# Attention and top-1 MoE in one kernel: first transfers in a fixed order, modality words by GpSimd, last keys' values two pairs at a time, and a planner's transfer figures fitted anew

## The chip, the cores and the metric

The kernel runs on one core of one Trainium2 chip. The metric is the device time of one execution in microseconds (us); the median of several runs is compared. A core has TensorE (PE, matrix products), VectorE (DVE), ScalarE (ACT), GpSimd (POOL) and SyncE (SP, which only issues DMAs and reads registers here). ACT and GpSimd can issue DMAs too.

## The reference

```python
scale = 1.0 / np.sqrt(64)                        # q, k, v: 8 x 8 heads x 576 x 64, tau = 0.02
scores = scale * np.matmul(q, k.transpose(0, 1, 3, 2))
thresh = np.max(scores, axis=-1, keepdims=True) - tau
scores = np.where(scores >= thresh, scores, -1000000000.0)
attn = np.exp(scores - np.max(scores, axis=-1, keepdims=True))
attn = attn / (np.sum(attn, axis=-1, keepdims=True) + 1e-09)
x = np.matmul(attn, v) ...                       # heads side by side: 4608 x 512
logits = x @ w_gate + modality_bias[modality_id] # 4608 x 8; modality_id is an 8-byte integer, 0 or 1
e_idx = np.argmax(logits, axis=1)
probs = np.exp(logits - logits.max(-1, keepdims=True))
probs /= probs.sum(-1, keepdims=True) + 1e-09
for e in range(8):                               # out = 0 before
    mask = e_idx == e
    h = np.maximum(x[mask] @ w1[e], 0.0)         # w1: 8 x 512 x 1024
    out[mask] = gate_w[mask, None] * (h @ w2[e]) # w2: 8 x 1024 x 512; gate_w = probs at e_idx
```

## The kernel before

The kernel has no order of its own in its text. Each step (an instruction or a few on one engine) is recorded in a `Plan` with its engine, an assumed duration, what it reads and writes, and a due time. `order()` then runs a list schedule through these assumed durations: on each engine the ready step that is due first goes next. The instructions are written out in that order, and each engine works through its own list strictly in order. Four figures, `LAND`, say how the planner expects a DMA to land: a lead, a pace for each unit of the transfer's size, a latency, and a floor for GpSimd's transfers. A transfer's size is given by hand as `us`, and every `load` takes 0.6 us of its issuing engine. `fill()` puts products of zeros where the plan expects TensorE to idle for over 0.6 us (L1435). A packed table of bytes, `SHIFTS`, moves each step's due time by up to 8 us either way; it has one byte for each step, so it belongs to one list of steps.

*Attention.* 64 heads are worked on as 32 pairs, each in 9 steps of 128 query rows: 288 steps. A step: TensorE makes the scores (L827) into one of two buffers `s` (576 keys, the last 64 of them from `nk` and `qb`); VectorE takes the row maximum `nm` (L836, L838); ACT takes the exponent `e` (L842); VectorE masks and sums to `pr` (L854); TensorE transposes `pr` (L880), ACT copies that to `ptm` (L883). The last 64 keys of two steps go through `rp` (copied by GpSimd, L867, or ACT) and `ptr` (L893, L900). TensorE multiplies with the values (L761): `v_m` holds 512 of a head's 576 rows of v, `vr` the last 64. For the first pair q and k come in parts, `raw` (512 rows of one head, halves of the columns) and `y` (the last 64 rows of both heads), transposed by TensorE (L768, L761, L787) and split by ACT and VectorE into high and low halves (`km`, `q`, L755, L757, L781, L783). Later pairs come as `kq`, are transposed on TensorE (L692) or VectorE, and are split by GpSimd (L727, L729, L749).

*Routing and experts.* After each batch the gate is computed, and a table of rows by expert, `tab`, is scattered. The words `modality_id` enter once, near the start: `xg` from DRAM, cast by VectorE to `y` (L644, L645). In the stream of attention stand 8 slots of expert work, and 4 more behind it: SyncE reads the expert's number and the rows (`tb`), GpSimd gathers rows of x (L1160, `xg`, `txg` behind the attention) and scales them (`xn`, L1182; VectorE behind the attention), TensorE transposes (L1187), SyncE loads weights (`raw`), GpSimd splits them (L1221, L1223), TensorE does both layers (L1239, L1271), ACT and VectorE hold the hidden layer's halves (`hh`, `hl` L1253), and GpSimd stores the result (L1290). Which slots are run behind the attention is computed on VectorE (L1060 to L1126, `le` and others).

All plain loads go through `load`, at L488. TensorE's results go to banks `bk`, `pm` or score buffers `s`; a matmul that reuses a bank waits until the bank's last reader is done.

## Time and profile before

| | us |
|---|---|
| runs | 999.27, 999.71, 1003.33 |
| median | 999.71 |
| profiled execution, its own time | 1002.75 |
| its span, first to last instruction | 1000.9 |
| busy: PE, DVE, ACT, POOL | 961.2, 747.2, 614.3, 593.8 |
| TensorE's mean granted clock | 0.988 |

Rows of the trace below come from the profiled execution. In a row of a time line the first number is the start, the second the length, then engine, line, operation, what it writes and reads, how many instructions stand together, and in brackets how long the engine had been idle before and what released it.

### The profile page before, as it was taken

Reading aid. Unit: us, or ns where it says so; the run is one execution under the profiler, and the core shown is the slowest. Engines: PE = TensorE matmul, PEld = TensorE weight load, DVE = VectorE, ACT = ScalarE, POOL = GpSimd, SP = SyncE. Lnnn points to the kernel's source line nnn. Section 1 sums busy time; section 2 is a strip of 40 time slices with the busy share of each in tenths; the row PEclk is TensorE's granted clock in tenths of the full one; section 3 lists DMA queues with packets and bytes.
Section 4 is the critical chain, followed back from the end, with each engine's and each line's share of the span. In section 5 each row is a group of like instructions: output and inputs, shape, how many; then the busy total and the mean of one; then the engine's idle time right before and its main releaser. Section 6 shows DMA issues by size and latency. Waiting matters only on the chain.

```text
span 1000.9 us, 19578 instructions
## 1 busy us (share of the span) xinstructions
PE 961.2 (96%) x6304; PEld 768.8 (77%) x6304; DVE 747.2 (75%) x1792; ACT 614.3 (61%) x1256; POOL 593.8 (59%) x746
## 2 busy tenths in 40 slices
...
GB/s 162 167 192 183 196 189 191 169 204 185 182 140 194 191 193 128 185 183 167 148 158 200 178 171 147 179 142 186 190 136 87 97 199 200 116 104 103 142 63 28
DMA packets 310448, 159.58 MB, mean 159 GB/s; under 512 B 235902, under 2 KB 281982, under 8 KB 308416
## 3 DMA queue, kind: packets, MB, share of 16 engines
...
q10 hardware_dynamic: 2112, 0.52, 0.2%
...
HBM read 85.98 MB, written 20.73 MB: 107 GB/s over the span
## 4 chain that ended last, share of the span: by engine, by line
PE 48%; DVE 5%; issue 3%; POOL 2%; ACT 1%; another core or an unknown queue 0%; POOLq 0%; ACTq 0%; DVEq 0%
PE bk L1239 11%; PE bk L1271 11%; PE bk L761 7%; PE s L827 7%; PE bk L880 5%; PE pm L1271 3%; PE pm L1239 1%; PE bk L1187 1%; DVE pr L854 1%; DVE nm L836 1%; DVE xn L1182 1%; DVE le L1090 1%; PE bk L893 1%; POOL out_dram L1290 0%; PE bk L961 0%
## 5 line engine op out<-in xcount | busy, mean ns | idle before, releaser
L842 ACT ACTIVATE e<-s,nm 128x576 f32<-128x576 f32 x288 | 213.9, 746 | 73.6 <-DVE nm L836 67.9
L854 DVE SCALAR_TENSOR_TENSOR pr<-s,nm,e 128x576 f32<-128x576 f32 x288 | 231.3, 812 | 28.8 <-ACT e L842 10.2
L836 DVE TENSOR_REDUCE nm<-s 128x1 f32<-128x576 f32 x288 | 214.8, 749 | 30.7 <-PE s L827 25.3
L827 PE MATMUL s<-km,q 128*128 128x288 f32 x1024 | 190.9, 313 | 7.0 <-DVE pr L854 5.0
L883 ACT COPY ptm<-bk 128x512 f32<-128x512 f32 x256 | 146.3, 592 | 45.3 <-PE bk L880 37.0
L827 PEld LDWEIGHTS s<-km,q 128*128 128x128 f32 x1024 | 147.5, 189 | 34.4 <-DVE pr L854 14.0
L880 PE MATMUL bk<-ident,pr 128*128 128x128 f32 x1152 | 166.4, 275 | 1.4 <-DVE hl L1253 1.4
L880 PEld LDWEIGHTS bk<-ident,pr 128*128 128x128 f32 x1152 | 136.6, 141 | 19.1 <-issue 2.9
L761 PE MATMUL bk<-ptm,v_m 128*64 128x256 f32 (+1 forms) x1024 | 139.7, 417 | 2.3 <-ACT ptr L900 2.3
L761 PEld LDWEIGHTS bk<-ptm,v_m 128*64 128x64 f32 x1024 | 69.2, 138 | 53.6 <-issue 11.1
L1253 DVE SCALAR_TENSOR_TENSOR hl<-bk,hh 128x512 fp32r<-128x512 f32 (+3 forms) x78 | 45.9, 591 | 64.3 <-ACT hh L1251 64.1
L1239 PE MATMUL bk<-xh,w1h 128*128 128x512 f32 (+2 forms) x240 | 89.7, 374 | 0.2
L729 POOL TENSOR_TENSOR q<-kqt,q 128x576 fp32r<-128x576 f32 x62 | 88.0, 1423 | 2.3
L1271 PE MATMUL bk<-w2h,hh 128*128 128x512 f32 x200 | 84.7, 423 | 0.0
L1239 PE MATMUL bk<-xh,w1l 128*128 128x512 f32 (+2 forms) x240 | 83.8, 349 | 0.4 <-POOL w1l L1223 0.4
L1223 POOL TENSOR_TENSOR w1l<-raw,w1h 128x512 fp32r<-128x512 f32 x64 | 82.3, 1288 | 2.9
L1239 PE MATMUL bk<-xl,w1h 128*128 128x512 f32 (+2 forms) x240 | 83.6, 348 | 0.0
L1223 POOL TENSOR_TENSOR w2l<-raw,w2h 128x512 fp32r<-128x512 f32 x64 | 81.9, 1284 | 2.2
L1271 PE MATMUL bk<-w2l,hh 128*128 128x512 f32 x200 | 79.5, 398 | 2.0 <-POOL w2l L1223 2.0
L727 POOL CAST q<-kqt 128x576 fp32r<-128x576 f32 x62 | 41.0, 668 | 65.0 <-PE s L827 36.7
L1271 PE MATMUL bk<-w2h,hl 128*128 128x512 f32 x200 | 79.1, 396 | 0.0
L1290 POOL DMA_INDIRECT out_dram<-y,tb x37 | 38.2, 1034 | 61.8 <-DVE y L1283 46.1
...
## 6 DMA issues: line engine op xcount, KB each, us to landing
raw<-in_moe_w_dram SPq DMA_DIRECT2D x128, 256.0 KB
...
```

What stands on the lines that cost most here:

```text
L729: op("POOL", 1.425, lambda s=s: nc.gpsimd.tensor_tensor(out=q2[:, 1, s], in0=kqt[:, s], in1=f32(q2[:, 0, s]), op=ALU.subtract), [kqt[:, s] ...
L761: nc.tensor.matmul(out=o, lhsT=lhsT, rhs=rhs, start=start, stop=stop, skip_group_check=True)
L827: nc.tensor.matmul(out=g.t[:, hf, 0:SH], lhsT=a, rhs=x, start=(z == 0), stop=(z == len(passes) - 1))
L836: op("DVE", 0.757, lambda: nc.vector.tensor_reduce(out=nm[:, 0, x:x + 1], in_=g.t[:, :, 0:SH], axis=AX.XY, op=ALU.max, negate=True), [g], ...
L842: op("ACT", 0.747, lambda: nc.scalar.activation(out=e, in_=g.t[:, :, 0:SH], func=AF.Exp, bias=nm[:, 0, x:x + 1]), [g, nm[:, 0, x:x + 1]], ...
L854: op("DVE", 0.826, lambda: nc.vector.scalar_tensor_tensor(out=pr.rearrange("p (a x) -> p a x", a=2), in0=g.t[:, :, 0:SH], scalar=nm[:, 1, ...
L880: op("PE", 0.44, lambda: [nc.tensor.transpose(out=g.t[:, kc * P:(kc + 1) * P], in_=pr[:, kc * P:(kc + 1) * P], identity=ident) for kc in r ...
L883: op("ACT", 0.583, lambda: nc.scalar.copy(out=o, in_=g.t.rearrange("a (k p) -> a k p", p=P)), [g], [o])
L1223: op("DVE" if d else "POOL", 0.686 if d else 1.29, lambda: (nc.vector if d else nc.gpsimd).tensor_tensor(out=lo.t, in0=raw.t, in1=f32(hi.t ...
L1239: nc.tensor.matmul(out=g.t[:, 0:WT], lhsT=a.t[:, cs], rhs=x.t[:, c, 0:WT], start=(c == 0 and y == 0), stop=(c == KC - 1 and y == 2))
L1253: op("DVE", 0.1 + 0.58 * WT / 512, lambda: nc.vector.scalar_tensor_tensor(out=hl.t[:, 0:WT], in0=g.t[:, 0:WT], scalar=0.0, in1=f32(hh.t[:, ...
L1271: nc.tensor.matmul(out=g.t, lhsT=a.t[:, ts], rhs=w.t, start=(y == 0 and i == 0), stop=(y == F2 - 1 and i == 2))
```

## The change

Four loads of `first` q and k parts by ACT and six by SyncE get due times of their own in the order in which they are written: k then q of the first head columns, then the few rows of k, then the second k and q parts, then the few rows of q. The modality words are loaded by GpSimd, in five transfers of one 4-byte word for each row (128 x 8 words), instead of nine by SyncE with both words of the 8 bytes. The last 64 rows of v come for two pairs in one transfer for each head of a pair: 32 transfers instead of 64. The planner's figures for landing, issuing and for some steps change, a wait `WAKE` is added where a SyncE instruction waits for a DMA, and `SHIFTS` is a new table.

```diff
-    LAND = (0.2, 1.05, 1.7, 4.5)
+    LAND = (0.0, 1.0, 1.95, 4.9)
+    WAKE = 0.7
...
+                x.soon = max(x.soon, fin + (self.NEXT if same else self.LAT).get(o.eng, 0.0 if same else 0.04)
+                                    + (self.WAKE if o.dma is not None and x.eng == "SP" else 0.0))
...
+    ISSUE = {0.1: 0.8, 0.2: 0.75, 0.6: 0.66, 0.95: 0.72, 1.3: 0.58, 2.6: 0.56}
+
     def load(out, in_, rd=(), wr=(), us=1.0, due=None, eng="SP"):
         q_ = {"SP": nc.sync, "ACT": nc.scalar, "POOL": nc.gpsimd}[eng]
-        op(eng, 0.6, lambda: q_.dma_start(out=out, in_=in_), rd, list(wr) or [out], dma=us, due=due)
+        op(eng, 1.0 if eng == "POOL" else 0.5 if eng == "ACT" else ISSUE.get(us, 0.65), lambda: q_.dma_start(out=out, in_=in_), rd, list(wr) or [out], dma=us, due=due)
...
-    vr2 = tiles(glob, 2, [P, 2, D], F32, "vr")
+    vr4 = keep(glob, [P, 4, D], F32, "vr")
...
+        turn_ = [20.0 * i - 260.0 for i in range(11, -1, -1)]
+
         def part(z, s, x, eng):
             load(first[z][s].t.rearrange("p (c x d) -> p c x d", c=NC, x=2)[:, :, x, :],
-                 (k, q)[z][0, s, 0:SA, :].rearrange("(c p) d -> p c d", c=NC), wr=[(first[z][s], x)], us=0.4, eng=eng)
+                 (k, q)[z][0, s, 0:SA, :].rearrange("(c p) d -> p c d", c=NC), wr=[(first[z][s], x)], us=0.5, eng=eng, due=turn_.pop())
...
-        mid_i = bi.t[:, 0:2 * B * NT].bitcast(I32).rearrange("p (b t two) -> p b t two", b=B, t=NT)
-        mid_v = mid.bitcast(I32).rearrange("(b s two) -> b s two", s=S, two=2)
-        for b in range(B):
-            load(mid_i[:, b, 0:NC, :], mid_v[b, 0:SA, :].rearrange("(c p) two -> p c two", c=NC), wr=[(bi, b)], us=0.4)
-        load(mid_i[:, :, NC, :], mid_v[:, S - P:S, :].rearrange("b p two -> p b two"), wr=[(bi, B)], us=0.7)
+        mid_i = bi.t[:, 0:B * NT].bitcast(I32).rearrange("p (b t) -> p b t", b=B)
+        mid_v = mid.bitcast(I32).rearrange("(b s two) -> b s two", s=S, two=2)[:, :, 0]
+        for t, o in enumerate([*range(0, SA, P), S - P]):
+            load(mid_i[:, :, t], mid_v[:, o:o + P].rearrange("b p -> p b"), wr=[(bi, t)], us=0.5, eng="POOL")
...
-            load(r[s * R:(s + 1) * R], sv[:, SA:S, :].rearrange("s r d -> r s d"), us=0.2)
+
+    def load_vr(p):
+        b, j = p // NPAIR, p % NPAIR
+        if p % 2 == 0:
+            for s in range(2):
+                load(vr4[s * R:(s + 1) * R], v[b, 2 * j:2 * j + 4, SA:S, :].rearrange("s r d -> r s d"), us=0.3)
...
-        op("DVE", 1.35, f1, [lg], [lt, mx])
-        op("DVE", 1.87, f2, [lt, iota_m, iota_x], [fe, mn, oh[:, 0:NT, :]])
+        op("DVE", 1.5, f1, [lg], [lt, mx])
+        op("DVE", 1.2, f2, [lt, iota_m, iota_x], [fe, mn, oh[:, 0:NT, :]])
...
-            op("SP", 0.4, f, keys, [(z, "e")])
+            op("SP", 1.0, f, keys, [(z, "e")])
...
-            op("SP", 0.9, f, keys + ["tab"] + [("tab", b, t) for b in range(nb) for t in range(NT)], [tb], dma=0.4)
+            op("SP", 1.7, f, keys + ["tab"] + [("tab", b, t) for b in range(nb) for t in range(NT)], [tb], dma=0.4)
...
-                eng, dur, e = ("DVE", 1.0, nc.vector) if xt_eng else ("POOL", 1.45, nc.gpsimd)
+                eng, dur, e = ("DVE", 0.77, nc.vector) if xt_eng else ("POOL", 1.2, nc.gpsimd)
...
-                op("SP", 0.42, g, late + [(z, "e")], [raw], dma=0.9)
+                op("SP", 0.65, g, late + [(z, "e")], [raw], dma=1.0)
...
+        at(t0 + 8, lambda p=p: load_vr(p))
...
-        c-k#iXCM^(1OA;&lvFaRH+d<QRgtnIA-i(6oITEV&Yowl<Lu+?jLx3fl7vzyTS}CfS=Qa}|9<#CAD)lTr)McYNexQ&vBBHo{d4OHHd=Oe&n%
+        c-j@!1w&K`+koL`&IAlG)F2^Uf^-f@NOw2V9Rmy?NOz}nr*t>cD1wb(V6N`kxd`Se;Q8L~`Vse?kxk1;$@EJtO)^S0;Vw<eO^eD+ipeXiN=y
```

Some 11 lines are added to the file, so a step that stood at L488 is at L493 after, L761 at L772, L827 at L838, L1182 at L1193 and L1271 at L1282. What the new order does is seen at three places.

The first place is the start. SyncE's first transfers (`raw_81` and `raw_82` hold k, `raw_83` and `raw_84` q, `y_113` and `y_114` the few last rows) are, before:

```order
L488 DMA y_113<-in_k_dram 64x2x64
L488 DMA raw_82<-in_k_dram 128x4x64
L488 DMA raw_83<-in_q_dram 128x4x64
L488 DMA y_114<-in_q_dram 64x2x64
L488 DMA raw_81<-in_k_dram 128x4x64
L488 DMA raw_84<-in_q_dram 128x4x64
```

and after:

```order
L493 DMA raw_81<-in_k_dram 128x4x64
L493 DMA raw_83<-in_q_dram 128x4x64
L493 DMA y_113<-in_k_dram 64x2x64
L493 DMA raw_82<-in_k_dram 128x4x64
L493 DMA raw_84<-in_q_dram 128x4x64
L493 DMA y_114<-in_q_dram 64x2x64
```

TensorE, behind its warm-up on zeros, before:

```order
L761 MATMUL bk_79<-ident,y_113 64x64 x2
L761 MATMUL bk_80<-ident,y_113 64x64 x2
L768 MATMUL bk_78<-ident,raw_83 128x128 x4
L768 MATMUL bk_77<-ident,raw_82 128x128 x4
L768 MATMUL bk_80<-ident,raw_81 128x128 x4
L787 MATMUL bk_79<-ident,y_114 128x64
L768 MATMUL bk_78<-ident,raw_84 128x128 x4
L827 MATMUL s_75<-km_164,q_162 128x288 x4
```

and after:

```order
L779 MATMUL bk_80<-ident,raw_81 128x128 x4
L779 MATMUL bk_79<-ident,raw_83 128x128 x4
L772 MATMUL bk_80<-ident,y_113 64x64 x2
L772 MATMUL bk_78<-ident,y_113 64x64 x2
L779 MATMUL bk_77<-ident,raw_82 128x128 x4
L798 MATMUL bk_79<-ident,y_114 128x64
L838 MATMUL s_75<-km_163,q_161 128x288 x4
L838 MATMUL s_76<-km_163,q_161 128x288 x4
```

The parts of k and q that the first scores read stand ahead of the few rows, and the second q part behind the scores (two rows further on). GpSimd's five word transfers stand ahead of its first copy of `rp`, in two pairs and a single one.

The second place is the second batch's slot of expert work on GpSimd. Before:

```order
L1160 DMA xg_101<-xs,tb_120 128x512
L1160 DMA xg_99<-xs,tb_120 128x512
L727 CAST q_163<-kqt 128x576
L1221 CAST w2h_91<-raw_81 128x512
L1160 DMA xg_100<-xs,tb_120 128x512
L729 TENSOR_TENSOR q_163<-kqt,q_163 128x576
L749 CAST nk<-km_164 64x576
L1182 TENSOR_TENSOR xn_102<-xg_101,tb_120 128x4x64 x2
L1290 DMA out_dram<-y_118,tb_119 4608x512
L1182 TENSOR_TENSOR xn_102<-xg_99,tb_120 128x4x64 x2
```

and after:

```order
L1171 DMA xg_101<-xs,tb_120 128x512
L1171 DMA xg_99<-xs,tb_120 128x512
L1171 DMA xg_100<-xs,tb_120 128x512
L738 CAST q_162<-kqt 128x576 x2
L760 CAST nk<-km_163 64x576
L740 TENSOR_TENSOR q_162<-kqt,q_162 128x576
L1193 TENSOR_TENSOR xn_102<-xg_101,tb_120 128x4x64 x2
L740 TENSOR_TENSOR q_162<-kqt,q_162 128x576
L1193 TENSOR_TENSOR xn_102<-xg_99,tb_120 128x4x64 x2
```

The three gathers now stand together, the second subtraction of `q` comes behind the first `xn`, and the store of an earlier result is not between the first two `xn`.

The third place is VectorE's part of the table of slots behind the attention. Before:

```order
L1085 TENSOR_TENSOR off<-off,ns 1x24
L1086 TENSOR_TENSOR off<-off,cum 1x24
L1090 TENSOR_TENSOR le<-ij,cum 1x88 x3
L1094 TENSOR_REDUCE ej<-le 1x33
L1098 TENSOR_SCALAR em<-ej 1x33
L1100 TENSOR_TENSOR le<-em,iota_m 1x88
L1102 TENSOR_TENSOR le<-le,off 1x88
L1253 SCALAR_TENSOR_TENSOR hl_111<-pm_9050,hh_107 128x512
L1100 TENSOR_TENSOR le<-em,iota_m 1x88
```

and after:

```order
L1096 TENSOR_TENSOR off<-off,ns 1x24
L1097 TENSOR_TENSOR off<-off,cum 1x24
L1101 TENSOR_TENSOR le<-ij,cum 1x88 x3
L1264 SCALAR_TENSOR_TENSOR hl_111<-bk_77,hh_107 128x512
L1105 TENSOR_REDUCE ej<-le 1x33
L1109 TENSOR_SCALAR em<-ej 1x33
L1111 TENSOR_TENSOR le<-em,iota_m 1x88
L1113 TENSOR_TENSOR le<-le,off 1x88
```

The step `hl_111`, which frees a bank, stands directly behind the three `le` now, where four small steps stood between.

## Rows read from the trace of the kernel before

**Rows 1.** The page, busy time of TensorE: us, share of the span, instructions.
```profile
PE 961.2 (96%) x6304; PEld 768.8 (77%) x6304; DVE 747.2 (75%) x1792; ACT 614.3 (61%) x1256; POOL 593.8 (59%) x746
```

**Rows 2.** Busy us by stretch: length, PE, PEld, DVE, ACT, POOL, clock, DMA share, GB/s.
```profile
0.00:25.00 25.00, 19.69 (x158) 17.02 (x158) 16.14 (x48) 15.22 (x31) 9.89 (x40) 1.00 0.75 162
25.00:125.00 100.00, 95.48 (x723) 69.71 (x724) 90.67 (x238) 72.64 (x133) 48.46 (x94) 1.00 0.86 185
760.00:860.00 100.00, 91.14 (x425) 70.25 (x424) 57.15 (x99) 27.30 (x49) 80.49 (x88) 0.95 0.52 144
```

**Rows 3.** TensorE's waits by releaser: us in total, times, the longest.
```profile
PE s L827 <- DVE pr L854: 6.1, 11, 1.3
...
PE bk L761 <- ACT ptr L900: 2.3, 1, 2.3
PE bk L893 <- POOL rp L867: 2.1, 1, 2.1
...
PE bk L692 <- DMA kq<-in_q_dram: 1.2, 1, 1.2
```

**Rows 4.** Time line of TensorE, start: us, us, instruction [idle before, releaser].
```profile
4.62 0.69 PE L761 MATMUL bk<-ident,y 64*64 64x64 f32 x8
7.05 2.79 PE L768 MATMUL bk<-ident,raw 128*128 128x128 f32 x12 [1.74 <-DMA raw<-in_q_dram]
...
10.07 1.10 PE L768 MATMUL bk<-ident,raw 128*128 128x128 f32 x4
11.15 1.44 PE L827 MATMUL s<-km,q 128*128 128x288 f32 x8
```

**Rows 5.** Time line of VectorE, start.
```profile
9.04 0.88 DVE L757 SCALAR_TENSOR_TENSOR q<-bk,gq,q 128x384 fp32r<-128x384 f32 x2 [2.73 <-ACT q L755]
```

**Rows 6.** Time lines of VectorE and then TensorE, 46 to 51 us.
```profile
46.87 1.35 DVE L644 CAST y<-xg 128x40 f32<-128x40 int32 x1 [0.73 <-DMA xg<-in_moe_modality_id_dram]
...
50.23 0.54 PE L827 MATMUL s<-km,q 128*128 128x288 f32 x2 [1.31 <-DVE pr L854]
```

**Rows 7.** Time line of GpSimd, start.
```profile
1.59 0.74 POOL L488 DMA_DIRECT2D tau_b<-in_tau_dram  x1 [0.15 <-issue]
...
15.30 1.27 POOL L727 CAST q<-kqt 128x576 fp32r<-128x576 f32 x2 [9.34 <-ACT kqt L695]
```

**Rows 8.** Time line of SyncE's DMA issues, 37 to 43 us.
```profile
37.47 0.65 SPq L488 DMA_DIRECT2D vr<-in_v_dram  x1
...
39.45 3.48 SPq L488 DMA_DIRECT2D xg<-in_moe_modality_id_dram  x3
```

**Rows 9.** Time lines of GpSimd and then TensorE, 213 to 223 us.
```profile
213.94 1.08 POOL L1160 DMA_INDIRECT xg<-xs,tb  x1 [0.16 <-DMA out_dram<-y,tb]
...
218.79 1.41 POOL L729 TENSOR_TENSOR q<-kqt,q 128x576 fp32r<-128x576 f32 x1
...
220.76 1.18 POOL L1182 TENSOR_TENSOR xn<-xg,tb 128x256 f32<-128x256 f32 x2
...
222.00 0.66 PE L1187 MATMUL bk<-ident,xn 128*128 128x128 f32 x4 [3.39 <-POOL xn L1182]
```

**Rows 10.** Time lines of VectorE, GpSimd and TensorE, 796 to 804 us.
```profile
796.42 5.63 DVE L1090 TENSOR_TENSOR le<-ij,cum 1x88 f32<-1x88 f32 x3
...
802.82 0.24 DVE L1100 TENSOR_TENSOR le<-em,iota_m 1x88 f32<-1x88 f32 x1
...
803.26 0.67 DVE L1253 SCALAR_TENSOR_TENSOR hl<-pm,hh 128x512 fp32r<-128x512 f32 x1
...
799.51 1.29 POOL L1223 TENSOR_TENSOR w1l<-raw,w1h 128x512 fp32r<-128x512 f32 x1
...
803.99 0.80 PE L1271 MATMUL pm<-w2h,hh 128*128 128x512 f32 x1 [3.13 <-DVE hl L1253]
```

**Rows 11.** Time lines of VectorE and then TensorE, 849 to 855 us.
```profile
849.18 5.35 DVE L1182 TENSOR_TENSOR xn<-txg,tb 128x256 f32<-128x256 f32 x2 [0.48 <-PE bk L1187]
...
854.59 1.11 PE L1187 MATMUL bk<-ident,xn 128*128 128x128 f32 x4 [3.30 <-DVE xn L1182]
```

More of the change, by code (lines that the diff above doesn't have):

```diff
@@ L255, in begin @@
                 same = x.eng == o.eng and o.dma is None
-                x.soon = max(x.soon, fin + (self.NEXT if same else self.LAT).get(o.eng, 0.0 if same else 0.04))
+                x.soon = max(x.soon, fin + (self.NEXT if same else self.LAT).get(o.eng, 0.0 if same else 0.04)
+                                    + (self.WAKE if o.dma is not None and x.eng == "SP" else 0.0))
                 x.left -= 1
@@ L292, in order @@
                         same = s.eng == o.eng and o.dma is None
-                        s.ready = max(s.ready, t + (self.NEXT if same else self.LAT).get(o.eng, 0.0 if same else 0.04))
+                        s.ready = max(s.ready, t + (self.NEXT if same else self.LAT).get(o.eng, 0.0 if same else 0.04)
+                                        + (self.WAKE if o.dma is not None and s.eng == "SP" else 0.0))
                         s.n -= 1
@@ L643, in f @@
         def f():
-            nc.vector.tensor_copy(out=mid_f[:, 1, :], in_=mid_i.rearrange("p b t two -> p (b t) two")[:, :, 0])
+            nc.vector.tensor_copy(out=mid_f[:, 1, :], in_=mid_i.rearrange("p b t -> p (b t)"))
             nc.vector.tensor_scalar(out=mid_f[:, 0, :], in0=mid_f[:, 1, :], scalar1=0.0, scalar2=None,
                                     op0=ALU.is_equal)
-        op("DVE", 0.8, f, [(bi, b) for b in range(B + 1)], [bf])
+        op("DVE", 0.8, f, [(bi, t) for t in range(NT)], [bf])
         for m, (t, key) in enumerate(((bias_t, bias_t), (bias_u, bu))):
@@ L653, in late_constants @@
            [bias_t, bu], [bias_t])
-        for b, xs_ in ((bx, [bx]), (bi, [(bi, b) for b in range(B + 1)])):
+        for b, xs_ in ((bx, [bx]), (bi, [(bi, t) for t in range(NT)])):
             op("POOL", 0.45, lambda b=b: nc.gpsimd.memset(b.t, 0.0), wr=xs_ + [b])
@@ L705, in load_v @@
         b, j = p // NPAIR, p % NPAIR
-        t, r = vm2[p % 2], vr2[p % 2]
+        t = vm2[p % 2]
         sv = v[b, 2 * j:2 * j + 2]
@@ L903, in pv @@
     def pv(p):
-        vt, vr = vm2[p % 2], vr2[p % 2]
+        vt, vr = vm2[p % 2], vr4[:, 2 * (p % 2):2 * (p % 2) + 2]
         ot = ot_[p % (NPAIR + 1)]
@@ new lines, in tile_attn_moe @@
+        |@>B;*eJNr*7+B@ZzX_#G&>k>#LK4*F~kZ%fZeoS=wF77r^Yu#vQa^^g|>_@kA{Ui2m=A?`XM9#+B$_Q?UEF@C90{;?jqp;`9JX^F1>ah3rq
+        PQa*MOk!Y6AAD%dEZs0I;mIXA@4Z=*)~tHQ5bNON*O%>ggsHc@K{ZslicCxEF)ADTt-PtJdPdB<?&;ZYb|X_)7u@$s)*obN)%p>nUk{%D&(3
+        inn68N9VbE2DtGmsZd223t?Etl`Zl_cJg_2GYeLC0l=XE}K=vB!q$vV{u@OJrqN@^1}BJ^esjyY(pIl}N_-3Tn(AH}pF7j=sm2*M&Z>7$KFb
+        QO$VUQu3V0UZ1)_7QF_(pFr(XyQ3s1R}|*TP~!0QA+S6U!ra3vCJU3Yw6yC1Q}IMqL4H7tX~8{$ACL?(&o9{C17HJ8Wz}k_EI)cdpee_*bFP
+        f2nntHwY~^Bxy84IPu+&sKq(dy#^VB<>a;KoXw5lnv-Iv!Mmoqc=&MYzQs)$9K2cb^?-F#g*ilT>oF#~ZjSZNXnOVpzGvk_VXRP%2xuI{!qx
@@ new lines, in tile_attn_moe @@
+        o2rV_bSbf1N6jB3?2jo!GJBkB?$!mPS;_6bJ%Y!$u8%KzyI;V?CT1@Zj*TE#4r^;Z+DVh`SA>{Ow+ONnehvjSNWwno=VzQ9CKke=HBABBB;-
+        +<it3;v(~l;_|5~OB4sqBn5RNLu!OuM4yKG`HQ|~F-!E9`63A~Tw~t(`5wYbk341}5N^;1;xAT$48IvLgV!KsKKFR!s}}k2HXNfzHHt#Bhsd
+        0~a!kn;oo1n9AQbQnNMGbyNYOfj55G=;Gz&m0QwZrgrX4VB;3k6*HgEl&M4-=@z=N;E$g#MBL0M!?zp_cN^n;p>skSnM<CDH%SdUJ4&~()`{
+        6MFs&Ojmycr|Sh?M`7#qA;L`+N_gMl&(&10V%#Q0Yd5~DKx;G8DhC4p$;*|5ZuI_DHE$j&<6{Hh^lx|1Rx<_55g;vvtUt13pNuXtj9w9Hyu1
+        sun~KhYM{`0zd8Mn-n*Z_|HVrCil!k)IH$d`(uy_u!Jit`vtqu+s01x%*Jdx3{KhLkJocJR?idmoGEK44Eht^Qnx)R{X)Jg$$khPI4}e66fY
@@ new lines, in tile_attn_moe @@
+        tTi0Ojxz_7F<SUiZUq4F8T{E!p!^@*E}D^g0O6C?bu4R3jn~3seG|4`Qp*U%@GlTH^<37!t}4EY8H_q@%cmyXbESFw_ey06#Z;;9C%6vB&ww
+        A(!vhMZWn(sX>fX;rTB1j>Es5%gI^h+VJw6iH2o6@c>0;9@)HPKRxLd#6?G$t)LGJTC*j+L_AgE_z^BgcfLRe>|bG*f+M|=`F=mR{Oo!l`o`
+        cI(?<L_P6t~bIxn!3Z}pXNPK0ae22yXupuR(3@L5NCDcD70tix0`QlLGZNf`$PH2^Mb?OJ>5UfLg>tBAnC4I_hzv7G309sM4R=h(7)+o*C$8
+        RhZ+k|m7HyozTFfLGC^>^1}^VDVc23>Q{}e^(!HyvW9RqE-A70N9gPS(x(>#SZ&aE9k4bi=b!@dg=Yh?w7~a8buwzE6CKih6o%#^8S_Os<I%
+        qqa6X^{J>C|S{1l?G<rhd8am^e&w;m~(HRADkp(31_-b*e&<!{Gt6$6&`KBlBNUUDl)A?O~IF>G*#U123JZbGMlI({JJ-_t?+=sDXmD7I{X`
```

125 lines of the change are left out of this document (54 added, 71 removed).

## The prediction

> **What bounds the kernel now.** I began with the engines' busy time: TensorE is busy 961.2 us, 96% of the span of 1000.9 [rows 1], so all that any change of order can win is what TensorE loses between its matmuls and after the last: about 40 us. The table by stretch of time says where [rows 2]. The first 25 us lose 5.3 us; from 25 to 125 us, 4.5 are lost, and there VectorE is at 90.67 of 100, so this stage is close to being bound by VectorE; the stretch 760:860, in which the attention has ended and the expert work is left, loses 8.9 us at a mean granted clock of 0.95. The list of TensorE's waits then gives names [rows 3], and its time line the places [rows 4, 9 to 11]: a few waits that occur once, each on another releaser: an xn of GpSimd (3.39 us), an xn of VectorE (3.30), an hl of VectorE (3.13), a ptr of ACT (2.3), an rp of GpSimd (2.1), the first part of q (1.74). Only the wait of the scores (L827) on pr recurs: 11 times, 6.1 us in all. A kernel whose order is planned from assumed durations stalls where an assumption is off by a few us, so I price the change by these places, one by one.
>
> **The change part by part.**
>
> *First transfers.* In the kernel before, the first real matmuls (the few rows of k) end at about 5.3 us, TensorE waits 1.74 us for the first part of q until 7.05, and the first scores run at 11.15 [rows 4]. So from the first part transposed to the first scores there are 11.15 - 7.05 = 4.1 us of ACT and VectorE steps. Both queues now send the parts of k and then q that scores 0 need ahead of everything else, and TensorE transposes them ahead of the few rows. What came first in the old order was in TensorE at 4.62 us, so I estimate that the first parts of k (larger than the few rows) are there at 4.8: the scores then start at 4.8 + 4.1 = 8.9, that is 2.25 us sooner. VectorE's work on q starts at 9.04 [rows 5], and its stage lasts to about 125 us at nine tenths busy [rows 2], so that what it starts sooner it ends sooner. Term: -2.25; bounds 0 (another part is late in its place) and -2.8 (the wait of 1.74 and 1.10 us of four transposes that now follow the scores).
>
> *Modality words.* Nine SyncE transfers become five on GpSimd, of 1024 separate 4-byte words each. What this removes: at 46.87 us VectorE had waited 0.73 us for the words and then spent 1.35 us on the cast, behind which TensorE waited 1.31 us for pr [rows 6]. In the new order the cast stands behind the eighth pr instead, some 25 us sooner, where VectorE is the bound too, so it still costs its own time, and only the wait and what the cast's stride costs can go. Term: -1.0; bounds -2.1 (0.73 + 1.35, all of it) and 0. What it adds: GpSimd's issue time. GpSimd is idle for 9.34 us before 15.30 us [rows 7], and the five stand there. The one plain transfer that GpSimd issues before, tau with 128 words, takes 0.74 us; a gather of 128 rows takes 1.08 [rows 9]. At 1.0 us each, five take 5.0 us inside the idle 9.34: nothing. At 0.74 us per 128 words they would take 8 x 0.74 = 5.9 us each, 29.6 in all, 20 us more than the cover, in front of the rp copies and q casts that the scores need. I take 1.0, since the two rows differ by far less than their bytes do; the upper bound is a rival below. The Trainium skill, "DMA: Bandwidth & Descriptors", section "Anatomy of one DMA", says that descriptor generation is small and variable and that many descriptors can be emitted before the cost shows; by it the five cost nothing beyond their 1.0, and no run here shows it yet.
>
> *SyncE.* Nine word transfers and, by loading the last keys' values for two pairs at once, 32 others go. Three of the word transfers take 3.48 us of SyncE's time, one vr load 0.65 [rows 8], so the loads queued behind the nine words go out up to 9 x 1.16 = 10.4 us sooner. But TensorE waits for such a load once (L692 on kq, 1.2 us [rows 3]), and a load that is hidden anyway wins nothing: term 0, bounds 0 and -1.2.
>
> *New order, second batch's slot.* GpSimd's xn started 6.82 us after the first gather had: two more gathers and the work on the next q stood ahead of it, and TensorE waited 3.39 us [rows 9]. In the new order the three gathers stand together and the second subtraction of q (1.41 us) is put behind xn, but three casts and a subtraction stay ahead, so GpSimd's own way from gather to xn is hardly shorter. What changes is that TensorE now has scores, transposes and l2 matmuls listed between gather and its transposes. Term: -2.0; bounds -3.4 and 0.
>
> *New order, the table of slots.* At 796.42 us three small tensor-tensor steps on VectorE (88 numbers each) take 5.63 us, while the same kind takes 0.24 a little later; GpSimd then runs casts and subtractions without a break. The hl behind them comes at 803.26, and TensorE, which needs its bank, loses 3.13 us [rows 10]. The planned figure of these steps is not touched. In the new order hl2 stands right behind the three; before, 803.26 - 802.05 = 1.2 us of small steps stood between. And the bank is asked for after 18 matmuls where it was 15, which I estimate at 0.6 us. So of 3.13 some 1.3 remain: term -1.8, bounds -3.1 and 0 (what GpSimd does beside it decides). The rule is in the Trainium skill, "SBUF — State Buffer", section "Who interferes with whom": a VectorE instruction with two SBUF inputs and a GpSimd instruction that reads SBUF exclude each other, and the loser waits whole instructions. The trace agrees (5.63 us for three, against 0.24). By that rule alone the stall depends on what GpSimd does just then, and the new figure for VectorE's xn speaks against the change.
>
> *New order, tail xn.* At 849.18 us two VectorE xn take 5.35 us, again beside GpSimd's work, and TensorE loses 3.30 us [rows 11]. The planner's figure for one goes from 1.0 to 0.77, away from these 2.7. In the new order six matmuls stand between the transposes of one chunk and the next, as before, and the two xn between them. Term: 0; bounds -3.3 and +1.
>
> *What a new order brings of its own.* The waits on ptr and rp, 2.3 and 2.1 us, came once each in 32 pairs of the same steps [rows 3]; a new order ends such waits and makes others. I count those two as drawn anew (0), and add 2.3 us, one such wait more, since the places improved above may be followed by others. The amount of matmuls and fillers is unchanged.
>
> **Sum.** -2.25 - 1.0 + 0 - 2.0 - 1.8 + 0 + 2.3 = -4.75 us. Against the profiled execution (1002.75 us, span 1000.9) this is 998.0; the median of the runs before is 999.71, 3.04 us under the profiled one, and against it 995.0. Half a per cent (5.0 us) is about what a measurement can tell from no change here: the three runs of before lie within 4.1 us.
>
> **The rivals.**
> *The stalls are only dealt anew* (0.24). The start wins 2.25, and new waits of two or three us each take it back. For it: nearly all waits of [rows 3] occur once. Against it: two of the figures that are changed (GpSimd's xn, the start of the transfers) lie at named stalls. Time: 998 to 1001.
> *Words by the piece* (slower, 0.08). GpSimd's transfer costs per word. 5 x 5.9 - 9.34 = 20 us late: 1015. It decides from (9.34 + 4.75) / 5 = 2.8 us for each on. Against it: 0.74 for 128 words and 1.08 for 128 rows of 2 KB differ little.
> *More blocked VectorE steps in the expert stage* (slower, 0.09). If xn (planned at 0.77) now meets GpSimd's work in four places of the stretch after 760 us where it was one, 3 x 3.3 = 9.9 us are lost, and at a clock of 0.95 [rows 2] the 100 us behind it some 2 more: 995.0 + 9.9 = 1005 to 1007. It decides from three such new waits on.
> *The fit removes most named waits* (0.14). -2.25, -1.3, -3.4, -3.3, -3.1 and half of ptr's and rp's 4.4 sum to -15.6: 984; with a third given back, 989.
> *My forecast* has the rest, 0.45: between 992 and 998.
>
> **How the numbers follow.** The range reaches from the half-won fit, 987, to the sum with three more waits of 3 us, 1004; outside lie the fullest fit (0.06), the words by the piece (0.08) and the worst of the expert stage (0.06). Faster by over 0.5% means under 994.7: the fit (0.14) and 0.65 of my own case, since more of its bounds lie below the sum than above (0.45 x 0.65 = 0.29): 0.43. Slower is 0.08 + 0.09 = 0.17. The rest, 0.40, is no change.
>
> **What would show it.** Right: the first scores near 8.9 us; no transfer of modality words on SyncE; five GpSimd issues near 1.0 us before 15 us; VectorE's cast without a wait before it; no wait of TensorE over 2 us on xn near 218 us; a wait of some 1.3 us on hl near 797, and one of about 3 us on a VectorE xn near 850. Wrong: first scores at 10.5 or later, GpSimd issues over 2.8 us or several new waits over 2 us in places that are not named here.

## The result and the profile after

The changed kernel takes 1004.26 us (median of 19 runs) beside 998.97 for the kernel before (19 runs on the same chip): ratio 1.0063, 95% interval 1.0044 to 1.0082, a loss of some 6 us. The ratio is that of the mean times, without one slow run of the kernel before (1552.37 us). The profiled execution took 1003.29 us with a span of 1001.6.

The page of the kernel after, busy time; it answers to [rows 1]:

```profile
PE 958.9 (96%) x6303; PEld 766.3 (77%) x6303; DVE 755.4 (75%) x1792; ACT 612.4 (61%) x1256; POOL 596.1 (60%) x751
```

The stretches of after, columns as in [rows 2], with the one that holds the end:

```profile
0.00:25.00 25.00, 19.93 (x151) 17.38 (x153) 17.17 (x50) 15.86 (x34) 16.59 (x47) 0.93 0.82 152
25.00:125.00 100.00, 95.26 (x737) 70.65 (x736) 92.39 (x238) 73.17 (x132) 48.25 (x95) 1.00 0.89 189
...
760.00:860.00 100.00, 90.82 (x418) 70.11 (x415) 55.69 (x100) 26.73 (x47) 81.99 (x89) 0.97 0.53 149
860.00:1001.60 141.60, 131.71 (x622) 109.48 (x621) 52.80 (x85) 44.57 (x81) 47.01 (x55) 0.98 0.30 91
```

In the first three TensorE is busy within 0.4 us of what it was. TensorE's waits of after, as in [rows 3]:

```profile
PE s L838 <- DVE pr L865: 9.8, 15, 1.7
PE bk L1198 <- DVE bj L1120: 3.7, 1, 3.7
PE bk L772 <- DVE oh L1015: 3.4, 3, 2.5
PE bk L1198 <- DVE xn L1193: 3.3, 1, 3.3
PE bk L1198 <- POOL xn L1193: 2.3, 3, 0.9
```

The waits that stood against hl (3.1), rp (2.1) and ptr (2.3) are gone or under 0.7; pr has 3.7 us more, and the waits put down to bj (read below) and oh are new. All listed waits sum to 31.9 us, where they were 32.3. TensorE's time line at the start, as in [rows 4]:

```profile
7.12 0.45 PE L772 MATMUL bk<-ident,y 64*64 64x64 f32 x8 [0.85 <-ACT km L792]
7.50 0.66 PE L779 MATMUL bk<-ident,raw 128*128 128x128 f32 x4
9.11 0.27 PE L798 MATMUL bk<-ident,y 64*128 64x64 f32 x1 [0.95 <-DVE q L768]
9.31 2.21 PE L838 MATMUL s<-km,q 128*128 128x288 f32 x8
```

The first scores start 1.84 us sooner, but their eight matmuls take 2.21 us where they took 1.44, in a stretch whose mean granted clock is 0.93. Time lines of GpSimd at the start and then of VectorE at the cast, as in [rows 6, 7]:

```profile
4.71 1.86 POOL L493 DMA_DIRECT2D xg<-in_moe_modality_id_dram  x2
...
7.38 0.88 POOL L493 DMA_DIRECT2D xg<-in_moe_modality_id_dram  x1
...
8.83 1.75 POOL L493 DMA_DIRECT2D xg<-in_moe_modality_id_dram  x2
13.94 0.24 POOL L878 COPY rp<-pr 128x64 f32<-128x64 f32 x1 [3.36 <-DVE pr L865]
...
26.57 1.07 DVE L650 CAST y<-xg 128x40 f32<-128x40 int32 x1
27.67 0.60 DVE L651 TENSOR_SCALAR y<-y 128x40 f32<-128x40 f32 x1
```

Five issues of about 0.9 us each, all before GpSimd waits anyway, and a cast that waits for nothing. Then the table of slots, VectorE and TensorE, as in [rows 10]:

```profile
797.36 2.44 DVE L1113 TENSOR_TENSOR le<-le,off 1x88 f32<-1x88 f32 x1
799.83 0.42 DVE L1117 TENSOR_REDUCE bj<-le 1x33 f32<-1x264 f32 x1
800.28 2.96 DVE L1118 TENSOR_TENSOR bj<-bj,ij 1x33 f32<-1x33 f32 x1
803.17 0.67 DVE L1264 SCALAR_TENSOR_TENSOR hl<-bk,hh 128x512 fp32r<-128x512 f32 x1
803.77 0.16 DVE L1120 TENSOR_SCALAR bj<-bj 1x33 f32<-1x33 f32 x1
...
803.99 0.63 PE L1198 MATMUL bk<-ident,xn 128*128 128x128 f32 x4 [3.67 <-DVE bj L1120]
```

The blocked steps are others of the same table, and TensorE waits 3.67 us instead of 3.13, at the same time of the program. The view puts this down to bj, which the transposes of xn do not read. In the same trace the record of their wait for VectorE starts at 803.88 us, after hl's semaphore update (803.85) and before bj's (803.94): what TensorE waits for is an hl again, a later one, which reads a bank and stands behind the blocked L1118. Last, the end, which the prediction did not price. TensorE's last instruction and GpSimd's last stores of after:

```profile
991.32 0.39 PE L1282 MATMUL pm<-tw2h,hl 128*128 128x512 f32 x1
992.07 0.98 POOL L1301 DMA_INDIRECT out_dram<-y,tb  x1 [3.90 <-DVE y L1294]
993.35 0.93 POOL L1301 DMA_INDIRECT out_dram<-y,tb  x1 [0.30 <-issue]
```

and of the kernel before, the same view:

```profile
994.26 0.99 POOL L1290 DMA_INDIRECT out_dram<-y,tb  x1 [3.29 <-issue]
995.58 0.93 POOL L1290 DMA_INDIRECT out_dram<-y,tb  x1 [0.33 <-DVE y L1283]
```

From the end of the last store to the end of the span are 1001.6 - 994.28 = 7.3 us; before, 1000.9 - 996.51 = 4.4. GpSimd's sequencer records in the same traces, which the views leave out, say what stands there: an instruction that signals for the software DMA queue, and then a drain. Their lengths, with GpSimd's transfers counted from its time line:

| kernel | GpSimd's transfers | one starts late: number | signal + drain, us | last matmul ends, us | span, us |
|---|---|---|---|---|---|
| before | 115 | 114th | 0.38 + 0.81 | 994.5 | 1000.9 |
| before_again | 115 | 114th | 0.38 + 0.81 | 989.0 | 995.4 |
| after | 120 | 83rd | 1.10 + 3.75 | 991.7 | 1001.6 |
| before_words_by_pool | 120 | 83rd | 1.10 + 3.75 | 994.2 | 1004.1 |
| before_plain_by_pool | 120 | 114th | 0.48 + 1.21 | 997.4 | 1004.4 |
| before_tau_by_sp | 114 | none | 2.47 + 9.38 | 987.9 | 1004.9 |
| before_tau_and_tail | 115 | 114th | 0.38 + 0.81 | 984.1 | 990.5 |
| after_words_by_sp | 115 | 114th | 0.38 + 0.81 | 1001.1 | 1008.9 |
| after_five_words_more | 125 | 83rd | 1.20 + 4.15 | 992.0 | 1002.5 |
| after_more_words | 130 | 83rd | 0.42 + 0.97 | 988.3 | 995.0 |

Signal and drain together grew by 4.85 - 1.19 = 3.66 us, over half of the loss.

### The profile page after: what moved, and what is told of

It reads as the page before. It is cut to its first block, busy times and chain, and to the rows that moved or that the text cites. A ratio compares the mean times of both kernels' runs of the same rounds, so it can differ in the third digit from the quotient of the medians.

```text
span 1001.6 us, 19573 instructions
## 1 busy us (share of the span) xinstructions
PE 958.9 (96%) x6303; PEld 766.3 (77%) x6303; DVE 755.4 (75%) x1792; ACT 612.4 (61%) x1256; POOL 596.1 (60%) x751
## 4 chain that ended last, share of the span: by engine, by line
PE 72%; DVE 11%; issue 5%; POOL 4%; ACT 3%; DMA 2%; SPq 2%; DVEq 0%; POOLq 0%; ACTq 0%
PE s L838 14%; PE bk L1282 14%; PE bk L772 13%; PE bk L1250 13%; PE bk L891 10%; DVE pr L865 3%; PE pm L1250 2%; PE pm L1282 2%; DVE nm L847 1%; PE bk L1198 1%; SPq L493 1%; PE bk L904 1%; ACT e L853 1%; PE bk L972 1%; ACT ptm L894 1%
## 5 line engine op out<-in xcount | busy, mean ns | idle before, releaser
L838 PE MATMUL s<-km,q 128*128 128x288 f32 x1024 | 193.7, 314 | 9.9 <-DVE pr L865 8.6
L838 PEld LDWEIGHTS s<-km,q 128*128 128x128 f32 x1024 | 146.8, 190 | 42.3 <-DVE pr L865 21.9
L772 PE MATMUL bk<-ptm,v_m 128*64 128x256 f32 (+1 forms) x1024 | 137.4, 412 | 0.3 <-issue 0.2
L772 PEld LDWEIGHTS bk<-ptm,v_m 128*64 128x64 f32 x1024 | 68.5, 136 | 49.8 <-issue 7.7
L1264 DVE SCALAR_TENSOR_TENSOR hl<-bk,hh 128x512 fp32r<-128x512 f32 (+3 forms) x74 | 43.1, 585 | 65.9 <-ACT hh L1262 64.8
L1262 ACT ACTIVATE hh<-bk 128x512 fp32r<-128x512 f32 (+3 forms) x74 | 38.5, 522 | 75.8 <-PE bk L1250 73.9
L1282 PE MATMUL bk<-w2h,hh 128*128 128x512 f32 x196 | 83.7, 427 | 0.6 <-DVE hl L1264 0.6
L880 ACT COPY rp<-pr 128x64 f32<-128x64 f32 x234 | 56.6, 253 | 43.0 <-DVE pr L865 38.7
L1282 PE MATMUL bk<-w2l,hh 128*128 128x512 f32 x196 | 78.3, 399 | 0.7 <-POOL w2l L1234 0.7
```

Of the source, the lines that this page charges most:

```text
L772: nc.tensor.matmul(out=o, lhsT=lhsT, rhs=rhs, start=start, stop=stop, skip_group_check=True)
L838: nc.tensor.matmul(out=g.t[:, hf, 0:SH], lhsT=a, rhs=x, start=(z == 0), stop=(z == len(passes) - 1))
L880: op("ACT", 0.248, lambda: nc.scalar.copy(out=o, in_=i), [i], [o])
L1282: nc.tensor.matmul(out=g.t, lhsT=a.t[:, ts], rhs=w.t, start=(y == 0 and i == 0), stop=(y == F2 - 1 and i == 2))
```

## The experiments

My first theories for the loss: the moved cast in the part that VectorE bounds; the end, lengthened by what GpSimd has done; and, as the rival, an order that only deals its stalls anew, with nothing else behind the loss. Ratios are to runs of before on the same chip.

**before_again.** The kernel before, unchanged.

> The kernel before, unchanged, for a second profile of it. Its first profiled execution was 1002.75 us where the median of its runs is 998.97, so a usual execution should hold some 4 us less of waits. Theory 'one sample' (the first profile shows it at a bad moment): 995 to 1000 us, the waits of TensorE shorter by about 4 us in sum, the same large ones (xn near 218 us, hl near 801 us, xn near 851 us) back at the same places. Rival 'same waits': all waits as in the first profile and the difference in the clock alone (granted clock higher than 0.988).

Ratio 0.9979 [0.9961, 0.9998]: nothing was changed and the interval leaves out 1, so a difference of 0.2% says nothing here. Its profile has a span of 995.4 us, 5.5 below the one that the prediction was worked from, and its wait on GpSimd's xn near 218 us is 1.1 us instead of 3.39 [rows 9], with one of 3.1 on rp instead; the 3.1 of hl and 3.3 of VectorE's xn recur. All its listed waits sum to 29.9 us (32.3 in the first profile), and its granted clock is 0.993 (0.988), so the theory and its rival both hold in part. Some waits in [rows 3] belong to the kernel, and others to one execution.

**after_pad.** More small GpSimd instructions, no transfer:

```diff
-        op("POOL", 0.1, lambda: nc.gpsimd.memset(l_[:, :, NE], 1e-9), wr=[l_[:, :, NE]])
+        op("POOL", 0.1, lambda: [nc.gpsimd.memset(l_[:, :, NE], 1e-9) for _ in range(9)], wr=[l_[:, :, NE]])
```

> The changed kernel with eight more small GpSimd memsets (of a constant that is set anyway) in GpSimd's idle time before 9 us; everything else in the same order. The end of the changed kernel's profile holds a GpSimd drain of 3.75 us where the kernel before has 0.81, and 7.3 us from the last store's issue to the end where it has 4.4. Theory 'end is a matter of where the program's code lies' (GpSimd's list is eight instructions longer now): drain back near 0.8, time some 3 us under the changed kernel's 1004.3, at 1001. Theory 'end is chance of one execution': drain anything from 0.8 to 3.8, time 1004 as the changed kernel. Theory 'end belongs to the order of the last stores': drain 3.7 again, time 1004.

1.0049 [1.0032, 1.0066], signal and drain still 1.10 + 3.75: the number of GpSimd's instructions is not it.

**after_castlate.** The two cast steps taken out of the order and put ahead of their first user (`res` is the order; the same for the `memset` behind them):

```diff
+        res = plan.fill(plan.order(4, marks["close"]), 4, idle)
+        late = [moved[0], moved[2]]
+        for i in late:
+            res.remove(i)
+        n = min(res.index(moved[0] + 1), res.index(moved[0] + 2))
+        res[n:n] = late
```

> The changed kernel with VectorE's cast of the modality words and the compare behind it moved from behind the eighth pr to just ahead of their first user (some eight steps later, about where the kernel before has it), and GpSimd's memset of that buffer moved along. Theory 'cast': the 2.3 us that the start wins are used up by this cast in the stage that VectorE bounds; then the ninth step's reduce starts at 26.1 instead of 27.8, TensorE has lost some 1.5 us less at 60 us, and the time is 1.5 us under the changed kernel, 1002.8. Rival 'deal' (the lead is lost in many small waits of the new order, not here): ninth reduce earlier, but the lead is gone again by 60 us and the time is 1004 as before.

1.0073 [1.0046, 1.0100]; the cast ran at 41.90 us and took 1.43, and nothing came back. The theory of the cast falls.

**after_jitter.** Each due time moved at random by nothing or a sixteenth:

```diff
+        g_ = random.Random(2)
+        for o in plan.ops:
+            o.due += g_.choice((-1, 0, 1)) / 16
```

> The changed kernel with every due time moved by -1/16, 0 or +1/16 us at random on top of the table: another order of the same steps; the planner's own end is 0.4 us later than with the table alone. Theory 'deal': unplanned waits are dealt by the order and the planner does not see them, so the time differs from the changed kernel's 1004.3 by several us in either sign (3 to 8), with the large single waits at other places. Theory 'plan': what the planner expects carries to the chip, so the time is within 1 us of the changed kernel's, 1003.5 to 1005.5.

1.0070 [1.0046, 1.0094]: another order of the same change, whose end the planner itself puts 0.4 us later, has the same loss and the same 1.10 + 3.75.

**after_words_by_sp.** The five word loads on SyncE, moved to stand ahead of the late cast of after_castlate, near 26 us:

```diff
-            load(mid_i[:, :, t], mid_v[:, o:o + P].rearrange("b p -> p b"), wr=[(bi, t)], us=0.5, eng="POOL")
+            load(mid_i[:, :, t], mid_v[:, o:o + P].rearrange("b p -> p b"), wr=[(bi, t)], us=0.5, eng="POOL", by="SP")
```

> The changed kernel with the cast of the modality words late (as in the run after_castlate) and the five word transfers issued by SyncE, standing together near 26 us of its list, instead of by GpSimd at the start; all other instructions in the same order. In the four profiles of the changed kernel and its variants the end of the program holds a GpSimd semaphore instruction of 1.10 us and a drain of 3.75 us, in the two of the kernel before 0.38 and 0.81: 3.66 us more. Theory 'words': GpSimd's word transfers lengthen its drain at the end of the program; then both instructions are back at 0.38 and 0.81 here, and the time is about 3.5 us under after_castlate's 1006.1, at 1002.5, though SyncE's loads behind the five may cost a us. Rival 'last stores' (the end is long because of the order of the last steps): 1.10 and 3.75 again, 1006.

1.0106 [1.0077, 1.0135], slower still, where some 3.5 us under after_castlate were expected. But the end is back at 0.38 + 0.81. A part of what it lost stands in TensorE's waits on SyncE's transfers, 4.5 us on three lines; after_castlate, from which it differs by the words alone, has 1.4. All listed waits sum to 36.9 us, and to 31.0 there:

```profile
PE bk L701 <- DMA kq<-in_k_dram: 2.8, 2, 1.6
...
PE bk L701 <- DMA kq<-in_q_dram: 0.9, 1, 0.9
...
PE bk L707 <- DMA kq<-in_k_dram: 0.8, 1, 0.8
```

**before_words_by_pool** and **before_plain_by_pool.** Five transfers more on GpSimd in the kernel before, into a place that nobody reads: 1024 words each in the first, the 128 words of `tau` each in the second.

```diff
+            for t, o in enumerate([*range(0, SA, P), S - P]):
+                nc.gpsimd.dma_start(out=bi.t[:, 200 + 8 * t:208 + 8 * t].bitcast(I32), in_=src[:, o:o + P].rearrange("b p -> p b"))
...
+            for t in range(5):
+                nc.gpsimd.dma_start(out=bi.t[:, 200 + 8 * t:201 + 8 * t], in_=tau.to_broadcast([P, 1]))
```

> The kernel before with five more GpSimd transfers of 1024 modality words each, written to unused columns of a buffer that is cleared later, in GpSimd's idle time before 15 us; nothing reads them. Theory 'words': the end grows by 3.66 us (1.10 and 3.75 instead of 0.38 and 0.81), the rest stays, so the time is 998.5 to 999.5 + 3.5 = 1002 to 1003. Rival 'last stores': end as in the kernel before, time unchanged within 1 us.

> The kernel before with five more plain GpSimd transfers as small as that of tau (128 words each, one for each partition), to the same unused columns. It tells whether the end grows with the number of GpSimd's plain transfers or with their words: theory 'per transfer': the end grows as with the 1024-word transfers, by 3 to 3.7 us, to 1002.5; theory 'per word' (an eighth of the words): it grows by about 0.45 us, time 999 to 1000; theory 'last stores': not at all.

1.0059 [1.0040, 1.0078] and 1.0065 [1.0044, 1.0086]. The first shows that the words alone make the end what it is after the change: 1.10 + 3.75. The second has as many transfers and an end of 0.48 + 1.21, as 'per word' had it (0.45 us more). But both are slower than expected, by ratio 5.9 and 6.5 us, though their ends differ by 3.16: the spare transfers cost something ahead of the end as well. VectorE's eighth pr in before, with the words and with the small ones:

```profile
27.92 0.81 DVE L854 SCALAR_TENSOR_TENSOR pr<-s,nm,e 128x576 f32<-128x576 f32 x1
...
29.53 0.81 DVE L859 SCALAR_TENSOR_TENSOR pr<-s,nm,e 128x576 f32<-128x576 f32 x1
...
31.54 0.81 DVE L858 SCALAR_TENSOR_TENSOR pr<-s,nm,e 128x576 f32<-128x576 f32 x1
```

So 1.6 and 3.6 us are lost at the start; TensorE waits there for kq, 1.0 and 1.5 us in the first run and 2.2 us at 14.77 us in the second. (The second run's profile also has a wait of 5.0 us on GpSimd's xn.) In the change, which was planned with its transfers, the eighth pr is not late: it starts at 25.83. What differs at the end can be seen far ahead of it. GpSimd's scatters of `tab` with 1024-word transfers in the program:

```profile
780.05 1.01 POOL L1038 DMA_INDIRECT tab<-pay,posi  x1 [0.30 <-DVE pk L1051]
782.45 0.98 POOL L1038 DMA_INDIRECT tab<-pay,posi  x1 [1.39 <-issue]
```

and the same two with 128-word transfers:

```profile
781.99 1.01 POOL L1037 DMA_INDIRECT tab<-pay,posi  x1 [0.30 <-DVE pk L1050]
783.30 0.97 POOL L1037 DMA_INDIRECT tab<-pay,posi  x1 [0.30 <-issue]
```

The 83rd transfer starts 1.09 us late in the one and not in the other; in the kernel before, it is the 114th that is late (the idle 3.29 above ends 1.75 us after the last `y` step that it stores). After has the same 1.40 at the same place:

```profile
777.10 0.98 POOL L1044 DMA_INDIRECT tab<-pay,posi  x1 [1.40 <-issue]
```

**before_tau_by_sp.** One GpSimd transfer fewer, the first:

```diff
-        load(tau_b, tau.to_broadcast([P, 1]), us=0.1, eng="POOL")
+        load(tau_b, tau.to_broadcast([P, 1]), us=0.1, eng="POOL", by="SP")
```

> The kernel before with its only plain GpSimd transfer, tau (128 words), issued by SyncE at the same place of the order. If plain GpSimd transfers lengthen the drain, the remaining 0.81 us may hold tau's part: theory 'per transfer': drain and semaphore instruction shorter by about 0.7 us, the time 0.5 us under the kernel before; theory 'per word': shorter by 0.1 us, time unchanged; a second thing, SyncE's first transfers come about 0.6 us later, could cost as much at the start.

1.0091 [1.0067, 1.0116]. Its matmuls end at 987.9 us, sooner than in either profile of before, and the end takes 11.85 us. The last store and the span:

```profile
988.97 0.93 POOL L1290 DMA_INDIRECT out_dram<-y,tb  x1 [1.81 <-DVE y L1283]
...
core 0: 1004.9 us, clock 0.988
```

15.0 us pass behind the last store, and no transfer starts late any more. Both theories had the end shorter; they are refuted.

**after_more_words** and **after_five_words_more.** Ten and five spare word transfers in the tail of the changed kernel, into a place that nobody reads any more (`n` counts back from GpSimd's last transfers; the second takes `pool[n:n + 1]`):

```diff
+            if i in pool[n:n + 2]:
+                for t in range(NT):
+                    nc.gpsimd.dma_start(out=bias_t[:, NT * (pool.index(i) - n) + t, :].bitcast(I32),
+                                        in_=words[:, t * R:t * R + P].rearrange("b p -> p b"))
```

> The changed kernel with ten more GpSimd transfers of 1024 words each, five and five, in GpSimd's idle time near 921 and 935 us, to a buffer that nothing reads any more. Theory 'lap': the end of the program (semaphore instruction and drain of GpSimd) grows in proportion to the descriptors of GpSimd's transfers since a lap of some fixed number began. From the runs: five 128-word transfers more make the drain 0.40 us longer, five 1024-word transfers 2.94 us, and taking one 128-word transfer away from the kernel before makes it 9.38, so the kernel before ends just behind the start of a lap, and a lap is worth 9.38 - 0.81 = 8.6 us. Ten more transfers make 0.81 + 15 x 0.588 = 9.63, minus the lap of 8.6: drain 1.1, semaphore instruction 0.45, and the time some 3.3 us under the changed kernel: 1001. Rival 'sum' (every word lengthens the end, and tau's absence did something else): drain 9.6, semaphore instruction 2.5, time 1011.

> As after_more_words, but five more transfers only, near 921 us. Theory 'lap' and rival 'sum' agree here: drain 3.75 + 2.94 = 6.7, semaphore instruction 1.8, time 3.7 us above the changed kernel: 1008. A rival 'early' (only transfers at the program's start lengthen its end): drain 3.75, time 1004.3.

Ten more transfers make it faster: 1.0017 [0.9997, 1.0038], with 0.42 + 0.97 at the end, near what 'lap' had. Five, on the same chip, give 1.0067 [1.0041, 1.0092], with 1.20 + 4.15. I had worked out 6.7 + 1.8 = 8.5 us for that end by words; by transfers it is 4.85 + 5 x 0.10 = 5.35, which is what it took. So the price by words in 'lap' is wrong, and that it came near for the ten is luck.

**before_tau_and_tail.** before_tau_by_sp with its one small transfer given back, in the tail:

```diff
+            if i == n:
+                nc.gpsimd.dma_start(out=gq, in_=tau.to_broadcast([P, 1]))
```

> The kernel before with tau's transfer issued by SyncE (as in before_tau_by_sp, where the drain was 9.38 us and the semaphore instruction 2.47) and one equally small GpSimd transfer in its place near 935 us, to a number that nothing reads any more. Theory 'lap': the count of GpSimd's descriptors is the old one, so the drain is 0.81 and the semaphore instruction 0.38 again; the matmuls end as in before_tau_by_sp (987.9 in its profile, against 994.5 and 989.0 in the two of the kernel before), so the time is 0 to 2 us under the kernel before: 997.5 to 999.5. Rival 'tau' (the long drain comes from the first transfer's change of engine): 9.38 again, 1008.

The end is 0.38 + 0.81 again, the 114th is late again, and 10.66 us are gone; the ratio is 0.9990 [0.9976, 1.0005]. Its profile has the shortest span of all, but the ratio does not tell it from the kernel before.

**before_jitter.** The kernel before with due times moved as in after_jitter (`random.Random(1)`).

> The kernel before with every due time moved by -1/16, 0 or +1/16 us at random on top of its table; the planner's own end is 7.0 us later by that. No transfer is added, so the drain stays 0.81. Theory 'plan': what the planner expects carries to the chip, so the time is 5 to 9 us above the kernel before, 1005 to 1008. Theory 'deal': the sum of the waits hardly depends on what the planner expects, 997 to 1002.

1.0123 [1.0103, 1.0144], with the end of before. The planner puts this order's own end 7.0 us later than that of before.

**before_first_order.** Of the change only the fixed order of the first transfers:

```diff
+        turn_ = [20.0 * i - 260.0 for i in range(11, -1, -1)]
...
+                 (k, q)[z][0, s, 0:SA, :].rearrange("(c p) d -> p c d", c=NC), wr=[(first[z][s], x)], us=0.4, eng=eng, due=turn_.pop())
...
```

> The kernel before with one part of the change alone: the first transfers get due times in the new fixed order (their sizes and all other figures as before); the table of shifts is the old one and the list of steps too, so the rest of the order is planned anew from it. No GpSimd transfer is added: the end stays at 4.4 us behind the last store. The planner's own end is 3.3 us later than the kernel before's. Theory 'start': first scores near 9.3 instead of 11.15 us and 2 us less in all: 0.998 of the kernel before. Theory 'plan': first scores near 9.3, but the time follows the planner's own end, 3 to 6 us above the kernel before: 1.003 to 1.006.

0.9995 [0.9980, 1.0010], although the first scores start at 9.12 us:

```profile
9.12 1.57 PE L829 MATMUL s<-km,q 128*128 128x288 f32 x8
```

The 2 us won at the start do not show in the time. In its profile the eighth pr starts 1.6 us sooner than in before and the twelfth 1.9 us later, for what follows the start was planned anew too; a wait of 2.7 us on kq near 111 us, 1.2 in the profile of before, is in its list.

**before_new_figures.** The planner's new figures with the old table, loads and first transfers:

```diff
-    LAND = (0.2, 1.05, 1.7, 4.5)
+    LAND = (0.0, 1.0, 1.95, 4.9)
+    WAKE = 0.7
...
```

> The kernel before with another part of the change alone: all the planner's figures of the change (landing, issue, WAKE, the steps' durations), with the old transfers and the old table of shifts, which was made for the old figures. No GpSimd transfer is added. The planner's own end is 965.7 by the new figures, where the old figures gave 946.6. Theory 'plan': a table that does not belong to the figures costs most of those 19 us on the chip: 1.010 to 1.020 of the kernel before. Theory 'fit' (figures nearer to the trace make a better order by themselves): 0.995 to 1.002. Theory 'deal': 1.002 to 1.008.

1.0211 [1.0180, 1.0242]; the planner puts it 19.1 us later. With the old table the new figures win nothing; figures and new table without the rest of the change were not run.

## Why the prediction was wrong

Forecast were 995.0 us and a gain of 4.75, that is 0.48%; measured is a loss of 0.63%, some 11 us apart. Two things failed. A cost at the end was left out (3.66 us by its records), and the gains at the start and in the new order did not come (the rest). The rival "the stalls are only dealt anew" describes the second, but its 998 to 1001 lacked the end. "More blocked VectorE steps" names 1005 to 1007, nearer in number, by luck: from 760 to 860 us TensorE loses 9.2 us where it lost 8.9, without the three new waits that it asks for. Most signs of being right came true (first scores, issues, cast, the wait near 218 us, that near 850); none of them looked at the end, and none was a measure of the whole.

**Modality words: the step that failed.** "Five take 5.0 us inside the idle 9.34: nothing." The issue was right (0.9 us each), and the rival of words by the piece is refuted. But a cost was left out, put at nothing without a reason: GpSimd's five transfers change how long signal and drain take at the end, by 3.66 us, in the change itself and with before_words_by_pool alone. By ratios, after against after_more_words, which has 3.46 of it removed, it is 0.46% or 4.6 us, each interval some 2 us to either side; on one chip, five spare transfers against ten are 0.50% apart, with ends that differ by 3.96 us. The prediction priced nothing behind the last store.

What the table shows of this: the end grows by 0.10 us with each transfer from the late one on. Five small transfers more behind the same late one cost 0.50 us both times (1.19 to 1.69, 4.85 to 5.35). The late one is the 2nd from the end in before and the 38th in after, and 36 x 0.10 = 3.6. Without a late one, all 114 seem to count: (11.85 - 1.19) / 112 is 0.095. The late one comes after 113 small transfers, or after 82 of which five have 1024 words: such a transfer fills as much as about seven small ones (36 / 5), though at the end it counts as one. My reading, which is not shown, is that a store of descriptors (the single orders of which a transfer is made up) is cleared whenever it is full, at the late transfer, and that the drain works through what came since. The counts fit it in nine of the ten rows, but no record names the store. The tenth, after_more_words, does not fit as it stands: its end of 1.39 us asks for a second clearing four transfers from the last, and by seven each its ten large ones make only some 104 to 106 small ones from the 83rd up to there, not 113. The Trainium skill, "DMA: Bandwidth & Descriptors", section "Anatomy of one DMA", says that many descriptors can be emitted before the cost shows: at the issue the trace agrees (0.74 us for 128 words, 0.9 for 1024); at the end of the program these runs show a price that the section does not have.

**First transfers, -2.25.** The mechanism was right (9.31 us; the forecast was near 8.9), the conclusion was not: "what it starts sooner it ends sooner". VectorE's eighth pr keeps 2.1 us of the lead, but the last matmul ends at 991.7 us, between the 994.5 and 989.0 of the two profiles of before. Before_first_order shows no gain with a lead of 2.03; its interval allows at most 2.0 us, and the rest of its order was planned anew. So the term is not shown, and 0, its bound, is nearest. TensorE's busy time in the first 25 us rose by 0.24 us only, and not all of it at full speed: TensorE was busy for 1.30 of the 3 us up to 9 us, and from 9 to 12 us the granted clock was 0.57 of full speed (1.2 GHz for most of it), where before and before_first_order have 1.00. That the first scores took 2.21 us is not shown to come of it, for before_again has 2.08 at 1.00.

**The cast, -1.0.** It waits for nothing and no pr stall stands behind it; after_castlate, with the cast elsewhere, finds no difference.

**SyncE, 0.** Nothing speaks against it; the loading of the last keys' values two pairs at a time was not tried alone.

**Second batch's slot, -2.0.** The wait of 3.39 us went, in the profile. But the unchanged kernel shows 1.1 to 3.4 there, so a term of this size was not the order's to win.

**Table of slots, -1.8.** It failed: the hl that was moved is on time (795.0 us), the steps L1113 and L1118 of the same table are blocked in place of the three le, and the next hl behind them holds TensorE for 3.67 us. The step as put, "of 3.13 some 1.3 remain", looked at one hl and one set of steps, not at what VectorE has listed next. The Trainium skill, "SBUF — State Buffer", section "Who interferes with whom", says that a VectorE instruction with two SBUF inputs and a GpSimd instruction that reads SBUF exclude each other; the trace agrees, with 2.44 and 2.96 us for two steps that take 0.24 and 0.18 us elsewhere, and GpSimd's casts and subtractions beside them from 797.84 to 803.19 us.

**Tail xn, 0.** Right: 3.3 us again, at 855.0 us where it was 854.6.

**A new order's own waits, +2.3.** Too small: pr 3.7 more, oh 3.4, 3.7 at the table, and 1.8 at the start on km and q; ptr and rp went as assumed. The sum of all is unchanged (31.9 against 32.3). After_more_words, with its end as in before to 0.2 us, gives the rest of the change, and with it whatever its ten spare transfers cost elsewhere: +1.7 us [-0.3, +3.8], where the sum had -4.75. The gains that were summed up are not there; how the rest splits over the steps stays open.
